# Attention and a feed-forward layer in one program: w_in's first half in two loads, fewer small matmuls and fp32 matmuls of zeros at the start, split 256-column matmuls in group 0, five chunks abreast in group 1

## The chip, the cores and the metric

The kernel runs on one core of one Trainium2 chip. The metric is the device time of one execution in microseconds; lower is better. Three timed runs of the kernel before took 325.07, 323.78 and 324.67 us (median 324.67). One more execution was recorded by the profiler.

## The reference

A block of attention with two paths, local and pooled, feeds a two-layer network with a gated activation.

```python
# attention: q, k, v are (8 batches, 8 heads, 576, 64)
q_d, k_d, v_d = (x.reshape(B, H, 144, 4, D).mean(axis=3) for x in (q, k, v))
out_d = softmax(scale * q_d @ k_d.T) @ v_d             # pooled, 144 x 144
out_up = np.repeat(out_d, 4, axis=2)                   # back to 576
mask = np.abs(pos[:, None] - pos[None, :]) < 4         # 7 neighbours
out_local = softmax(where(mask, scale * q @ k.T, -1e9)) @ v
x = (out_up + out_local).transpose(0, 2, 1, 3).reshape(4608, 512)
# network: w_in (512, 2048), w_out (2048, 512)
h = x @ w_in
out = (h * sigmoid(1.702 * h)) @ w_out                 # (4608, 512), float32
```

## The kernel before

The order of every instruction is written by hand (`manual_schedule`): each engine runs its instructions in the order of the program text, and waits on semaphores where a tile is not ready. The framework derives these waits from the regions that instructions read and write.

The 4608 tokens are worked in nine groups of 512 (`TG`). For each group, `mm1` (matmuls at L766, `hps_mm`) makes 16 chunks of 128 hidden units, each the sum of four products over the four blocks of 128 input channels (`dmc`); ScalarE applies SiLU (L777) from PSUM into `gT`. `mm2` (L846) then makes four blocks of 128 tokens, each the sum of 16 products with `w_out`; ScalarE scales them (L829) and SyncE stores them. The attention of batch g + 1 is woven into group g: a table of positions (`POS`, for group 0 `POS_0`) says ahead of which of the group's steps the pieces of `attention(b)` are issued. Each head pair hp fills block hp of the transposed activations, `xT[hp]`.

PSUM has three double tiles `PA[0..2]` (two banks each) and two single ones `PM[0..1]`; `PB` is `PA` in another order. `two` lists the six banks of `PA`, so `two[4]` and `two[5]` are the halves of `PA[2]`. `bank` in `mm1` names the bank of each chunk; the first `abreast` chunks of a group are made side by side, block by block, so that the last block of `xT` is needed late.

Batch 0's attention runs alone ahead of group 0 and in another form. GpSimd (POOL) issues the loads in this order, on one queue: k and q of batch 0, v in ten pieces (`load_vb`), `w_in` in two halves of 1024 columns (L239), k and q of batch 1, half of `w_out`, and later v of batch 1 and the rest. TensorE warms up with matmuls of zeros (`warm`, L733), makes local scores (L374) and pooled scores (L419) for head pairs 0/1 and then 2/3, pools v with selection matrices (`prep_vd_pe`, L339), and for each head pair multiplies the local weights with v (`av_local0`, L452) and the pooled ones with pooled v (`av_down0`, L468). VectorE divides by the sums (`normalise0`, L488 to L495). `turned` up-samples and transposes the result on TensorE (`transp_sum`, L510 and L527) and copies it into `xT` (`copy_x`). Between the turnings of head pairs stand the first matmuls of group 0's first product, written as `part(chunks, blocks)`: chunks 0 and 1 of block 0 behind the turning of pair 1, block 1 of the same chunks behind that of pair 2, and so on. A weight tile of chunk f takes every second column of 256 columns: chunks 0 and 1 read columns 0 to 255 of `w_in`.

In group 0's `mm2` the token blocks are worked in an order of their own: blocks 0 and 1 into `PM`, blocks 2 and 3 into the halves of `PB[0]`, four hidden chunks at a time. The pieces of batch 1's attention stand there at steps 0 (scores of the first head quad), 12 (scores of the second), 20 (`prep_vd_pe` for batch 1), 24, 33, 42 and 51 (`avx1` for each head pair, L557 and L569). For later batches pooled v comes from GpSimd (`prep_v4`, L311 and L314), from loads that SyncE issues, and `avx` (L634, L656) does two head pairs at once.

The functions that the change touches, and what calls them, follow with the line numbers of the profile.

Of the kernel before, what the change touches and what calls it, by code (L numbers as in the profile page):

```python
# [8 lines left out]
FP32 = mybir.dt.float32  # L9
# [6 lines left out]
TG = 512  # L16
# [3 lines left out]
def kernel(  # L20
# [9 lines left out]
    nc = tc.nc  # L30
# [207 lines left out]
    def load_w_in(c, n):  # L238
        nc.gpsimd.dma_start(  # L239
            out=w_in_bf[:, :, c : c + n],  # L240
            in_=bass.AP(
                tensor=moe_w_in.tensor, offset=moe_w_in.offset + c,
                ap=[[d_ff, 128], [128 * d_ff, n_dmc], [1, n]],
            ),
        )
# [213 lines left out]

    def av_down0(hp, o):  # L460
        Ed, vd, u = eds[hp // 2], vds[0], hp % 2
        blocks = [(0, 3)] + [(kc, c) for c in (0, 2) for kc in range(3)]
        for kc, c in blocks:
            rows, pos, slot, q0 = {
                0: (128, 0, 6, SD * kc), 2: (64, 1, 4, SD * kc + 128), 3: (64, 1, 5, 0),
            }[c]
            for j in range(2):
                nc.tensor.matmul(  # L468
                    o[64 * pos : 64 * pos + rows, j, 65 * slot : 65 * slot + 65],
                    lhsT=Ed[64 * j : 64 * j + 48, u, q0 : q0 + rows],  # L470
                    rhs=vd[64 * j : 64 * j + 48, kc, hp, :],
                    start=(kc == 0), stop=(kc == 2 or c == 3),
                    tile_position=(64 * j, 64 * pos),
                )

# [8 lines left out]
    def normalise0(o, y, parts="ab"):  # L484
        yl, yd, rc = y
        ov = o[:, :, 0:455].rearrange("p x (c e) -> p x c e", e=65)
        c0, c1 = {"a": (0, 4), "b": (4, 7), "ab": (0, 7)}[parts]
        nc.vector.reciprocal(rc[:, :, c0:c1], ov[:, :, c0:c1, 64:65])  # L488
        if "b" in parts:
            nc.vector.tensor_tensor(  # L490
                out=yd.rearrange("p s x d -> p x s d"), in0=ov[:, :, 4:7:2, 0:D],
                in1=rc[:, :, 4:7:2].to_broadcast([128, 2, 2, D]), op=ALU.mult,
            )
            c1 = 6
        nc.vector.tensor_tensor(  # L495
            out=yl[:, :, c0:c1], in0=ov[:, :, c0:c1, 0:D],
            in1=rc[:, :, c0:c1].to_broadcast([128, 2, c1 - c0, D]), op=ALU.mult,
        )
# [231 lines left out]
    def warm(n, cols=512, t=None):  # L730
        t = pm_tile() if t is None else t
        for _ in range(n):
            nc.tensor.matmul(  # L733
                t[:, 0:cols], lhsT=wz[:, 0:128], rhs=wz[:, 0:cols], start=True, stop=True
            )

    def attention(b):
        st = {}

        def s_pe(qd):  # L740
            P = PB if b == 1 else PA
            st["d", qd], st["s", qd] = scores_mixed(b, qd, P)

        def s_act(qd):
            if qd == 0:
                nc.scalar.preload_act_table_set("natural_log_exp_and_others")
            if qd:
                exp_down(qd, st["d", qd])
            exp_local(qd, st["s", qd], (1, 0) if qd else (0, 1))
            if not qd:  # L750
                exp_down(qd, st["d", qd])
            mask_local(qd)

        def s1():
            s_pe(1)
            s_act(1)

        first = [lambda: s_pe(0), lambda: s_act(0), s1]
        if b == 1:
            return first + [lambda hp=hp: avx1(b, hp) for hp in range(HP)]  # L760
        return first + [lambda: avx(b, (0, 1)), lambda: avx(b, (2, 3))]
# [1 line left out]
    w_in_v = w_in_bf.rearrange("p c (f i u) -> p c f u i", u=2, i=128)  # L763

    def hps_mm(g, ffc, dmc, acc):
        nc.tensor.matmul(  # L766
            acc,
            lhsT=w_in_v[:, dmc, ffc // 2, ffc % 2, :],
            rhs=xT[dmc][:, g * TG : g * TG + TG],
            start=(dmc == 0), stop=(dmc == n_dmc - 1),  # L770
        )

    def new_gT():
        return moe_sb.tile([128, n_ffc, TG], BF16, name="gT", tag="gT")
# [6 lines left out]
    def mm1(g, gT, steps):  # L781
        two = [PA[i][:, u, :] for i in range(3) for u in range(2)]
        bank, abreast = [PM[0], two[0], PM[1], two[2], two[4]], 4
        if g == 0:
            bank = acc[0:6] + late
        elif g == 1:
            bank, abreast = [two[0], two[2], two[1], two[3], PM[1], PM[0]], 6
            bank = bank + [two[4], two[5], two[0], two[2]] + PM + PM + PM
        else:
            bank = bank + bank + PM + PM + PM  # L790
        for ffc in range(n_ffc):
            for f in steps.get(ffc, ()):
                f()
            if g and ffc < abreast:
                if ffc == 0:
                    for dmcs in ((0, 1), (2,), (3,)):
                        for u in range(abreast):
                            for dmc in dmcs:
                                hps_mm(g, u, dmc, bank[u])
            elif g or ffc > 5:  # L800
                for dmc in range(n_dmc):
                    hps_mm(g, ffc, dmc, bank[ffc])
            else:
                continue
            silu(gT, ffc, bank[ffc])

    def mm2(g, gT, steps):
# [28 lines left out]
        for t, ffc in order:  # L836
            if g == n_groups - 1 and t == 3:
                continue
            for f in steps.get(n, ()):
                f()  # L840
            n += 1
            if ffc == 0:
                ops[t] = PB[0][:, t - 2, :] if g == 0 and t > 1 else pm_tile()
            wide = d_model // 2 if g == 0 and t > 1 and ffc > 7 else d_model
            for c in range(0, d_model, wide):
                nc.tensor.matmul(  # L846
                    ops[t][:, c : c + wide],
                    lhsT=gT[:, ffc, t * 128 : (t + 1) * 128],
                    rhs=w_out_bf[:, ffc, c : c + wide],
                    start=(ffc == 0), stop=(ffc == n_ffc - 1 and c + wide == d_model),  # L850
                )
            if ffc == n_ffc - 1 and not (g == 0 and t == 2):
                for u in (2, 3) if g == 0 and t == 3 else (t,):
                    store(u, ops[u], 0, d_model, nc.scalar, nc.sync)
# [35 lines left out]
    fill()  # L890
    for i in range(5):
        load_vb(0, i)
    load_w_in(0, 1024)
    load_w_in(1024, 1024)
    for qd in range(NQ):
        load_qk(1, qd)
# [17 lines left out]
    reduce_qk(0, 1, "k")  # L914
    reduce_qk(0, 1, "q")
    warm(6)
    warm(10, 128)
    exp_down(0, scores_d(0, 0, PA[2]))
    sp = scores(0, 1, barred=True, sp=PA[0:2])
    exp_local(1, sp)  # L920
# [1 line left out]
    for hp in range(4):  # L922
# [1 line left out]
        y[hp] = y_tiles0()  # L924
    prep_vd_pe(
        0, PM[0], range(0, 2),
        between=lambda kc, i: warm({(1, 2): 1, (1, 3): 2}.get((kc, i), 0), t=PM[1]),
    )
    for hp in range(2):
        av_local0(hp, o[hp], range(4))  # L930
# [1 line left out]
    sd = scores_d(0, 1, PB[2])  # L932
    prep_vd_pe(0, PM[1], range(2, 3))
    exp_down(1, sd)
    warm(2, t=PM[0])
    nc.scalar.preload_act_table_set("silu_and_others")
    for hp in range(3):
        av_local0(hp, o[hp], range(4 if hp < 2 else 0, 5))
        av_down0(hp, o[hp])
        normalise0(o[hp], y[hp], "b" if hp < 2 else "ab")  # L940
    make_mask()

    gT0 = new_gT()
# [100 lines left out]
```

## Time and profile before

| | |
|---|---|
| timed runs | 323.78, 324.67, 325.07 us |
| profiled execution | 323.4 us |
| its span, first to last instruction | 321.6 us |
| matmuls busy (PE) | 309.9 us, 96% of the span |
| ScalarE (ACT) busy | 203.1 us, 63% |
| VectorE (DVE) busy | 146.9 us, 46% |
| GpSimd (POOL) busy | 149.5 us, 46% |
| mean granted TensorE clock | 0.988 |
| all DMA | 39.96 MB, mean 124 GB/s |

How to read the rows. A row of the timeline has the start of a run of like instructions, its length, the engine, the source line, the operation, output and inputs, the shape and the count; a bracket at its end holds the idle time of that engine just before the row and what ended it. "issue" stands where the profile shows nothing that the engine waited for. PEld is TensorE's weight load, which overlaps its matmuls. Matmuls are pipelined: the next starts before the one before has ended, so the length of one is more than its share of the time, and a gap between ends and starts is less than what start to start would show. A row of the table of stretches has the stretch, its length, then busy time and number of instructions of PE, PEld, DVE, ACT and POOL, the granted TensorE clock, the DMA share and GB/s. `pa` and `pm` are the tiles of `PA` and `PM`.

By stage: batch 0's attention fills TensorE's first 25 us; group 0 runs from there to about 65 us, with batch 1's attention within; from 74 us TensorE is busy without a gap of note until 300 us; the last group has no attention beside it and ends with the stores.

### The profile page before, as it was taken

The numbers are of one execution on the slowest core, as the hardware profiler recorded it, in microseconds if no ns is written. First come the engines' busy times: TensorE is split into PE (matmuls) and PEld (weight loads), VectorE is DVE, ScalarE is ACT, GpSimd is POOL, SyncE is SP. The second block draws the span as 40 slices with busy tenths as digits, with TensorE's granted clock in tenths as the row PEclk, the third lists the DMA queues.
The fourth block names the chain that finished last, engine by engine and source line by source line (L and its number), as shares of the span: only waits on it lengthen the run. The fifth ranks groups of instructions, "written<-read, shape, count | busy, mean of one in ns | idle before, by whom it ended". The sixth has DMA issues, their size and how long they took to land.

```text
span 321.6 us, 9884 instructions
## 1 busy us (share of the span) xinstructions
PE 309.9 (96%) x4303; PEld 156.7 (49%) x4303; DVE 146.9 (46%) x300; ACT 203.1 (63%) x324; POOL 149.5 (46%) x173
## 2 busy tenths in 40 slices
PE   8879998998999999999999999999999999999995
PEld 3554454644554555454545454445444544444444
DVE  6862922782279226922693269325941580000000
ACT  4452775575885688567857785778587857415611
POOL 8832380447512992299229932992299030000000
PEclk9995999999999999999999999999999999999999
DMA  7999999649933893379438942894240120020011
GB/s 124 119 207 211 169 145 211 120 154 204 192 111 115 172 204 105 106 169 198 124 99 178 196 122 89 176 194 123 91 137 2 42 93 2 0 98 35 0 65 65
DMA packets 62571, 39.96 MB, mean 124 GB/s; under 512 B 44608, under 2 KB 51904, under 8 KB 62528
## 3 DMA queue, kind: packets, MB, share of 16 engines
q0 software_dynamic: 17312, 14.95, 33.1%
q1 hardware_dynamic: 45072, 24.32, 29.0%
q8 instruction: 33, 0.54, 0.8%
q14 instruction: 10, 0.08, 0.1%
q10 hardware_dynamic: 144, 0.07, 0.1%
HBM read 44.83 MB, written 9.44 MB: 169 GB/s over the span
## 4 chain that ended last, share of the span: by engine, by line
PE 89%; DMA 6%; POOL 2%; ACT 1%; issue 1%; DVE 0%; POOLq 0%
PE pm L846 36%; PE pm L766 24%; PE pa L766 15%; DMA w_in_bf<-in_moe_w_in_dram 4%; PE pa L392 3%; PE pa L846 2%; PE pa L656 2%; DMA qb<-in_q_dram 2%; PE pa L634 2%; PE pa L419 2%; ACT gT L777 1%; PE pm L861 1%; POOL vb L216 1%; PE pa L569 1%; PE pa L557 0%
## 5 line engine op out<-in xcount | busy, mean ns | idle before, releaser
L846 PE MATMUL pm<-w_out_bf,gT 128*128 128x512 bf16 x528 | 119.6, 379 | 1.1 <-issue 1.1
L766 PEld LDWEIGHTS <-w_in_bf 128*128 128x128 bf16 x576 | 55.8, 98 | 69.3 <-issue 3.4
L766 PE MATMUL pm<-xT,w_in_bf 128*128 128x512 bf16 x348 | 89.0, 382 | 0.4 <-DMA w_in_bf<-in_moe_w_in_dram 0.4
L846 PEld LDWEIGHTS <-gT 128*128 128x128 bf16 x576 | 54.3, 98 | 62.4 <-issue 1.6
L777 ACT ACTIVATE gT<-pm 128x512 bf16<-128x512 f32 x87 | 52.1, 604 | 40.9 <-PE pm L766 40.9
L766 PE MATMUL pa<-xT,w_in_bf 128*128 128x512 bf16 x228 | 60.5, 381 | 2.1 <-ACT gT L777 2.1
L444 DVE TENSOR_TENSOR es<-es,mask 128x600 bf16<-128x600 bf16 x28 | 17.7, 668 | 92.7 <-ACT es L430 92.5
L829 ACT ACTIVATE osb<-pm 128x512 f32<-128x512 f32 (+2 forms) x35 | 20.3, 582 | 30.5 <-PE pm L846 28.0
L777 ACT ACTIVATE gT<-pa 128x512 bf16<-128x512 f32 x57 | 32.9, 608 | 8.6 <-PE pa L766 8.6
L726 POOL TENSOR_TENSOR xT<-xT,od 128x576 bf16<-128x576 bf16 x12 | 15.4, 1281 | 40.8 <-DVE xT L710 40.8
L710 DVE TENSOR_TENSOR xT<-n,l 128x285 bf16<-128x285 f32 (+1 forms) x96 | 28.1, 365 | 0.0
L294 POOL TENSOR_TENSOR pq<-kT 128x576 f32<-128x576 bf16 x11 | 12.7, 1157 | 30.4 <-DVE kT L263 30.4
L311 POOL TENSOR_TENSOR pq<-v 112x512 f32<-112x512 f32 x18 | 23.9, 1331 | 4.9 <-DMA v<-in_v_dram 4.9
L831 DVE TENSOR_SCALAR osb<-pm 128x128 f32<-128x128 f32 x1 | 0.3, 291 | 54.0 <-ACT osb L829 54.0
L216 POOL DMA_DIRECT2D vb<-in_v_dram x20 | 13.7, 698 | 16.4 <-DVE y L490 4.7
L430 ACT ACTIVATE es<-pa 128x600 bf16<-128x600 f32 x32 | 19.7, 669 | 1.8 <-PE pa L374 1.7
L263 DVE STREAM_TRANSPOSE kT<-kb 128x576 f32<-128x576 f32 x16 | 19.9, 1245 | 0.0
L263 DVE STREAM_TRANSPOSE qT<-qb 128x576 f32<-128x576 f32 x16 | 19.8, 1238 | 0.0
L436 ACT ACTIVATE ed<-pa 128x864 bf16<-128x864 f32 x16 | 14.3, 894 | 5.9 <-PE pa L419 5.9
L705 ACT ACTIVATE l<-l 128x1440 f32<-128x1440 f32 x12 | 16.9, 1404 | 0.4
L699 ACT ACTIVATE l<-pa 128x492 f32<-128x492 f32 x24 | 12.6, 578 | 6.0 <-PE pa L656 6.0
L700 DVE COPY n<-pa 128x492 f32<-128x492 f32 x24 | 15.0, 665 | 2.8 <-ACT l L699 2.2
(119 smaller groups left out, 361.2 us busy)
## 6 DMA issues: line engine op xcount, KB each, us to landing
out_dram<-osb SPq DMA_DIRECT2D x34, 256.0 KB, 2.0
vf<-in_v_dram SPq DMA_DIRECT2D x60, 128.0 KB, 5.3
v<-in_v_dram SPq DMA_DIRECT2D x72, 96.0 KB, 3.0
kb<-in_k_dram POOLq DMA_DIRECT2D x16, 288.0 KB, 6.6
qb<-in_q_dram POOLq DMA_DIRECT2D x16, 288.0 KB, 8.5
w_in_bf<-in_moe_w_in_dram POOLq DMA_DIRECT2D x2, 1024.0 KB, 11.7
w_out_bf<-in_moe_w_out_dram POOLq DMA_DIRECT2D x4, 512.0 KB, 13.6
vb<-in_v_dram POOLq DMA_DIRECT2D x20, 64.0 KB, 5.8
```

The costliest lines, as they stand in the source:

```text
L216: nc.gpsimd.dma_start(out=vbs[b % 2][64 * par : 64 * par + 64, i, :, 0:D], in_=bass.AP(tensor=v.tensor, offset=v[b, 0].offset + (114 * i + ...
L263: nc.vector.transpose(out=t32.rearrange("p (i c) -> p c i", c=18), in_=store[b, qd].bitcast(FP32).rearrange("p (c d) -> p c d", c=18),)
L311: eng.tensor_tensor(out=t1[0:112], in0=x[:, :, 0:2, :], in1=x[:, :, 2:4, :], op=ALU.add)
L430: nc.scalar.activation(out=es[2 * qd + u][:, :, 0:300], in_=sp[u][:, :, 0:300], func=AF.Exp, scale=inv_sqrt_d,)
L444: nc.vector.tensor_tensor(out=ev, in0=ev, in1=mask, op=ALU.mult)
L705: nc.scalar.activation(out=l, in_=l, func=AF.Exp, scale=-1.0)
L710: nc.vector.tensor_tensor(out=out, in0=sub(n, *part), in1=sub(l, *part), op=ALU.mult)
L726: eng.tensor_tensor(out=xs, in0=xs, in1=sub(od[:, u, :], 0, (1, SD), (0, 4)), op=ALU.add)
L766: nc.tensor.matmul(acc, lhsT=w_in_v[:, dmc, ffc // 2, ffc % 2, :], rhs=xT[dmc][:, g * TG : g * TG + TG], start=(dmc == 0), stop=(dmc == n_ ...
L777: nc.scalar.activation(out=gT[:, ffc, :], in_=acc, func=AF.Silu, scale=GELU_SCALE)
L829: eng.activation(out=osb, in_=ap, func=AF.Copy, scale=1.0 / GELU_SCALE)
L846: nc.tensor.matmul(ops[t][:, c : c + wide], lhsT=gT[:, ffc, t * 128 : (t + 1) * 128], rhs=w_out_bf[:, ffc, c : c + wide], start=(ffc == 0) ...
```

## The change

Seven edits, made together:

- `w_in`'s first half is loaded as two loads of 512 columns; the second half stays one load of 1024. Ten loads follow one place further back on GpSimd.
- `av_down0` makes 12 matmuls for head pairs 0 to 2 instead of 14: the separate pair for slot 5 (which only puts numbers where nobody has written) goes, and the three pairs for slot 4 write slot 5 with it (130 columns instead of 65). Pair 3 keeps 14.
- `warm(10, 128)`, `warm(2, t=PM[0])` and the three warming matmuls of 512 columns inside `prep_vd_pe` go.
- `fill_pe(n, t)` is new: n matmuls of zeros, with the zero tile read as fp32, 128 x 128 by 256 columns. One stands inside `prep_vd_pe`, two behind the third head pair's `av_down0`.
- In group 0 the first product's chunks 6, 7 and 8 make their blocks 1 to 3 as two matmuls of 256 columns each instead of one of 512.
- In group 0 the second product does the same for hidden chunks 8 to 15 of token blocks 0 and 1; blocks 2 and 3 did so before.
- Group 1 makes five chunks abreast instead of six, and chunk 5 onwards takes other banks: `PM[0], two[4], two[0], two[2], PM[1], PM[0], ...` instead of `PM[0], two[4], two[5], two[0], two[2], PM[0], ...`.

```diff
     def av_down0(hp, o):
         Ed, vd, u = eds[hp // 2], vds[0], hp % 2
-        blocks = [(0, 3)] + [(kc, c) for c in (0, 2) for kc in range(3)]
-        for kc, c in blocks:
-            rows, pos, slot, q0 = {
-                0: (128, 0, 6, SD * kc), 2: (64, 1, 4, SD * kc + 128), 3: (64, 1, 5, 0),
-            }[c]
+        last = hp == HP - 1
+        blocks = [(0, 5)] if last else []
+        blocks += [(kc, slot) for slot in (6, 4) for kc in range(3)]
+        for kc, slot in blocks:
+            rows, pos, q0 = (128, 0, SD * kc) if slot == 6 else (64, 1, SD * kc + 128)
+            n = 2 if slot == 4 and not last else 1
             for j in range(2):
                 nc.tensor.matmul(
-                    o[64 * pos : 64 * pos + rows, j, 65 * slot : 65 * slot + 65],
+                    o[64 * pos : 64 * pos + rows, j, 65 * slot : 65 * (slot + n)],
                     lhsT=Ed[64 * j : 64 * j + 48, u, q0 : q0 + rows],
-                    rhs=vd[64 * j : 64 * j + 48, kc, hp, :],
-                    start=(kc == 0), stop=(kc == 2 or c == 3),
+                    rhs=vd[64 * j : 64 * j + 48, kc, hp : hp + n, :],
+                    start=(kc == 0), stop=(kc == 2 or slot == 5),
...
+    def fill_pe(n, t):
+        z = wz.bitcast(FP32)
+        for _ in range(n):
+            nc.tensor.matmul(t[:, 0:256], lhsT=z[:, 0:128], rhs=z, start=True, stop=True)
+
...
     def hps_mm(g, ffc, dmc, acc):
-        nc.tensor.matmul(
-            acc,
-            lhsT=w_in_v[:, dmc, ffc // 2, ffc % 2, :],
-            rhs=xT[dmc][:, g * TG : g * TG + TG],
-            start=(dmc == 0), stop=(dmc == n_dmc - 1),
-        )
+        n = TG // 2 if g == 0 and 5 < ffc < 9 and dmc else TG
+        for c in range(0, TG, n):
+            nc.tensor.matmul(
+                acc[:, c : c + n],
+                lhsT=w_in_v[:, dmc, ffc // 2, ffc % 2, :],
+                rhs=xT[dmc][:, g * TG + c : g * TG + c + n],
+                start=(dmc == 0), stop=(dmc == n_dmc - 1 and c + n == TG),
+            )
...
         elif g == 1:
-            bank, abreast = [two[0], two[2], two[1], two[3], PM[1], PM[0]], 6
-            bank = bank + [two[4], two[5], two[0], two[2]] + PM + PM + PM
+            bank, abreast = [two[0], two[2], two[1], two[3], PM[1]], 5
+            bank = bank + [PM[0], two[4], two[0], two[2]] + PM[::-1] * 4
...
-            wide = d_model // 2 if g == 0 and t > 1 and ffc > 7 else d_model
+            wide = d_model // 2 if g == 0 and ffc > 7 else d_model
...
-    load_w_in(0, 1024)
+    load_w_in(0, 512)
+    load_w_in(512, 512)
     load_w_in(1024, 1024)
...
     warm(6)
-    warm(10, 128)
     exp_down(0, scores_d(0, 0, PA[2]))
...
     prep_vd_pe(
         0, PM[0], range(0, 2),
-        between=lambda kc, i: warm({(1, 2): 1, (1, 3): 2}.get((kc, i), 0), t=PM[1]),
+        between=lambda kc, i: fill_pe(int((kc, i) == (1, 3)), PM[1]),
     )
...
     exp_down(1, sd)
-    warm(2, t=PM[0])
     nc.scalar.preload_act_table_set("silu_and_others")
     for hp in range(3):
         av_local0(hp, o[hp], range(4 if hp < 2 else 0, 5))
         av_down0(hp, o[hp])
         normalise0(o[hp], y[hp], "b" if hp < 2 else "ab")
+    fill_pe(2, PM[0])
     make_mask()
```

## The prediction

> **What bounds the kernel now.** I read the page first, then TensorE's timeline to 80 us, then a table of stretches, then the rows of the loads and of the engines that release TensorE.
>
> ```profile
> span 321.6 us, 9884 instructions
> PE 309.9 (96%) x4303; PEld 156.7 (49%) x4303; DVE 146.9 (46%) x300; ACT 203.1 (63%) x324; POOL 149.5 (46%) x173
> ...
> q8 instruction: 33, 0.54, 0.8%
> ```
>
> TensorE sets the end. Its program is 4303 weight loads and 4303 matmuls. The instruction queue moved 0.54 MB in 33 pieces, 261 instructions a piece by division, so near 128 pairs of load and matmul. The gaps worth removing are the bracketed ones here:
>
> ```profile
> 14.36 0.49 PE L733 MATMUL pm<-wz 128*128 128x256 bf16 x3 [0.41 <-issue]
> ...
> 21.37 0.22 PE L452 MATMUL pa<-vb,es 64*64 64x65 bf16 x4 [1.74 <-issue]
> 21.40 0.22 PE L468 MATMUL pa<-vd,ed 48*64 48x65 bf16 x2
> ...
> 21.97 0.63 PE L510 MATMUL pm<-up,y 128*128 128x231 bf16 x4
> ...
> 22.92 0.35 PE L452 MATMUL pa<-vb,es 64*64 64x65 bf16 x18
> ...
> 23.65 0.69 PE L510 MATMUL pa<-up,y 128*128 128x231 bf16 x4
> ...
> 27.67 1.04 PE L766 MATMUL pm<-xT,w_in_bf 128*128 128x512 bf16 x2 [0.42 <-DMA w_in_bf<-in_moe_w_in_dram]
> ...
> 44.52 2.76 PE L846 MATMUL pm<-w_out_bf,gT 128*128 128x512 bf16 x12
> ...
> 48.26 0.60 PE L846 MATMUL pm<-w_out_bf,gT 128*128 128x512 bf16 x2
> 49.99 0.59 PE L846 MATMUL pm<-w_out_bf,gT 128*128 128x512 bf16 x2 [1.13 <-issue]
> 50.42 1.02 PE L846 MATMUL pa<-w_out_bf,gT 128*128 128x512 bf16 x4
> ...
> 70.68 1.03 PE L766 MATMUL pa<-xT,w_in_bf 128*128 128x512 bf16 x4
> 73.82 2.75 PE L766 MATMUL pa<-xT,w_in_bf 128*128 128x512 bf16 x12 [2.11 <-ACT gT L777]
> ```
>
> Three gaps have no releaser ("issue"). The table of stretches cut at them counts the matmuls between:
>
> ```profile
> 0.00:14.10 14.10, 11.57 (x223) 6.04 (x224) 11.33 (x34) 6.44 (x10) 12.28 (x28) 1.00 1.53 126
> 14.10:20.50 6.40, 5.28 (x128) 2.87 (x128) 4.20 (x10) 4.04 (x7) 4.12 (x7) 1.00 1.19 169
> 20.50:49.50 29.00, 27.07 (x384) 14.03 (x384) 14.31 (x20) 16.31 (x33) 13.04 (x17) 0.88 1.31 181
> ```
>
> 223, then 128, then 384 = 3 x 128. So I take "issue" to be TensorE at the end of one program piece, with the next not there; pieces end after matmuls 223 + 128k. A piece ends wherever the count says, so added and removed matmuls move the ends through the code. After a stall the next piece was there 21.37 - 14.36 = 7.0 us later; the piece after that lasted longer and cost nothing.
>
> The clock comes on top (the last three numbers of a row are granted clock, DMA share and GB/s):
>
> ```profile
> 17.27:24.10 6.83, 5.09 (x145) 3.35 (x134) 5.15 (x14) 3.92 (x8) 2.00 (x3) 1.00 1.12 210
> 24.10:27.51 3.41, 3.15 (x21) 1.68 (x21) 1.23 (x2) 0.98 (x4) 0.00 (x0) 0.50 1.12 211
> 27.51:30.92 3.41, 3.25 (x16) 1.57 (x17) 0.00 (x0) 0.54 (x3) 1.61 (x3) 0.50 1.11 211
> 71.89:78.71 6.82, 4.89 (x76) 2.33 (x77) 2.19 (x2) 4.64 (x9) 6.74 (x8) 1.00 0.94 196
> ```
>
> From 24.10 to 30.92 TensorE ran at half clock, after a stretch with 1.74 us idle and mostly small matmuls. The stretch around the 2.11 us gap, as idle but with dense matmuls, kept the full clock.
>
> The price list, start to start: a 512-column matmul (2.76 - 0.38)/11 = 0.216 us, taking 0.38 as the length of one; a 256-column one (0.49 - 0.27)/2 = 0.11. A gap counts about 0.17 more than its bracket, since TensorE could have started the next matmul 0.17 before the previous one's modelled end.
>
> **The change, part by part.**
>
> *w_in in three loads.* The chain of waits and the rows of the tile:
>
> ```profile
> L239 POOL DMA_DIRECT2D w_in_bf<-in_moe_w_in_dram x2: 792/798/803, 13.1 to 13.9; - x2
> ...
> DMA to landing us min/median/max: 9.6/11.7/13.8
> ...
> 13.86 13.76 DMA w_in_bf<-in_moe_w_in_dram
> ...
> 30.89 0.57 PE pa L766 x2
> ```
>
> The first half landed 9.6 us after 13.1, at 22.7; the second at 27.63. Yet what waits to 27.67 is the pair of block 1 for chunks 0 and 1, columns 0 to 255, which lie in the first half; the block 0 pair had run before the second half landed. So the wait covers more than the columns it needs: in each partition the second load spans from column 1024 of block 0 to the end of block 3, and block 1 lies between. All three new loads span block 1 too. I therefore expect the wait to remain, on the last third, and the split to give nothing. It costs one more issue on POOL (0.80 us), behind which the next k/q, w_out and v loads are issued; the transfers are queued behind each other, so their landing is set by the rate. Rates: 210 GB/s in the stretch of w_in, 126 in that of the small v packets (first row above). For 1 MB in halved packets the bounds are 0 and 8.3 - 5.0 = 3.3 us; I take 0.3, near the w_in end, as half-size packets are nearer to it. TensorE resumes at 27.97.
>
> *The start.* Out go 10 + 3 + 2 warming matmuls and 2 in each of three head pairs; in comes one fp32 matmul, later two. The 10 lie ahead of a wait for VectorE, the fp32 one ahead of a v load, and the third head pair behind ScalarE's reading of its bank:
>
> ```profile
> 11.73 0.58 PE L419 MATMUL pa<-qdT,kdT 32*64 32x144 bf16 x24 [0.64 <-DVE qdT L282]
> ...
> 16.35 0.11 PEld L339 LDWEIGHTS <-psel 128*64 128x64 bf16 x2 [0.45 <-DMA vb<-in_v_dram]
> ...
> 18.20 0.90 ACT L436 ACTIVATE ed<-pa 128x864 bf16<-128x864 f32 x1
> ```
>
> So nothing starts earlier up to 19.1. The piece that ended 14 matmuls into the third pair's 34 (the 371st ends it) now ends at 371 - 21 + 1 = 351, exactly behind it; TensorE does 0.6 us of work (21.37 to 21.97) before the stall instead of behind it. The fp32 matmuls stand at that edge. The trace has none; 256 fp32 columns are at least a 256-column bf16 matmul, 0.11, and I bound it above by four times a 512-column step at half clock, 4 x 2 x 0.216 = 1.7; value 0.45, two of them 0.9. The Trainium skill ("FP8 and Floating Point Precision", TensorE Precision Notes) says true FP32 takes four passes through the array; by it one is an estimated 4 x 0.11 = 0.44, and the sum would be the same. Even at the upper bound they are nearly covered: the work from 21.4 to the w_in wait (up-sampling and turning of pairs 0, 1, 2 at 22.92 - 21.97 = 0.95 each, the last pair's products at 23.65 - 22.92 = 0.73, two dense matmuls at 0.43) is 4.0 us at full clock, so TensorE reaches it at 25.4 and idles 2.5 us.
>
> What is gained is the clock. Before, 27.67 to 30.89 ran at half clock: four dense matmuls and the last turning, 3.22 us. At full clock they are 4 x 0.216 + 0.95 (21.97 to 22.92) = 1.81. With fewer idle us in 17 to 24 I expect full clock there: 3.22 - 1.81 - 0.3 = **1.1 us**. If not, -0.3.
>
> *Group 0's split matmuls.* 9 in the first product, 16 in the second; a pair of 256 columns is 2 x 0.11, so nothing, at most 25 x 0.01 = 0.2. But they and the start move the piece's end that cost 1.13: it stood two matmuls behind the scores, at 735; now 733 - 21 + 1 + 2 + 9 = 724 ends the scores, and 11 more fit, eight dense ones and three small instead of two dense: 6 x 0.216 + 0.2 = 1.5 us later in the code, against a loss of 1.13 + 0.17 = 1.3. The stall goes; next late is ScalarE's reading of the bank of the first `pa` product:
>
> ```profile
> 48.43 0.89 ACT L436 ACTIVATE ed<-pa 128x864 bf16<-128x864 f32 x1 [0.92 <-PE pa L419]
> ```
>
> It ends at 49.32, so that product starts at 49.37 instead of 50.42: **1.05 us** (0 to 1.3).
>
> *Group 1.* The seventh chunk's bank shares its PSUM tile with the eighth's:
>
> ```profile
> 70.23 2.06 ACT L777 ACTIVATE gT<-pa 128x512 bf16<-128x512 f32 x4 [1.64 <-PE pa L766]
> 72.15 1.12 ACT L777 ACTIVATE gT<-pm 128x512 bf16<-128x512 f32 x2
> 73.11 0.66 ACT L777 ACTIVATE gT<-pa 128x512 bf16<-128x512 f32 x1
> ```
>
> The seventh SiLU ends at 73.77 and TensorE starts at 73.82: the eighth chunk's writes wait for the reading of the same tile's other half. With five abreast, `two[0]`'s tile is complete at the group's 18th matmul (17 x 0.216 + 0.38 = 4.1 us after its start) instead of the 21st, SiLUs follow at 0.5 each, and the eighth chunk goes into `two[0]`: SiLU 0 to 2 are done at 5.6, TensorE asks behind 28 matmuls, at 6.05. The gap (2.28 start to start) goes. But what is fed by DMA does not come earlier by it:
>
> ```profile
> 87.23 0.84 POOL L314 TENSOR_TENSOR vd<-pq 112x256 bf16<-112x256 f32 x1
> ...
> 89.48 0.26 PE L634 MATMUL pa<-ed,vd 48*64 48x144 bf16 x4
> 89.56 0.23 PE L634 MATMUL pa<-ed,ones 48*64 48x144 bf16 x4
> ```
>
> The third block of pooled v is ready at 88.07 and needed 0.15 behind 89.48; moved up 2.28 that is 87.35, so 0.75 is lost again: **1.5 us** (1.3 to 2.28; -0.5 if the bank turns themselves wait).
>
> **The sum.** 1.1 + 1.05 + 1.5 = 3.65. The profiled execution took 323.4 (span 321.6 and 1.8 around it) and lies 1.3 below the median, 324.67; the mean of it and the three timed is 324.2. From 324.2: **320.6**; its own range 319.2 to 321.9.
>
> **The rivals.**
>
> - *The w_in wait is freed.* For: the first two loads land near 22.7. Against: block 1 waits on columns that it doesn't read. TensorE goes on at 25.4, 2.5 us more: 318.1.
> - *The clock stays half to 30.92.* For: less dense work in 10 to 17. The 1.1 becomes -0.3: 322.0.
> - *The half clock moves into the dense stage.* The 2.5 us idle ahead of w_in are one gap; if the gate answers at 30.92 and holds 6.83 us as before, 3.4 us of dense work are lost: 324.0. Against: the row 71.89:78.71. The Trainium skill ("TensorE: Matmul & The Clock Gate", Why this matters for your kernels) allows gaps up to about 3 us; by it no drop follows here. The trace half agrees: 2.11 did no harm, 1.74 among small matmuls did.
> - *A stall stays.* The program piece after 724 comes late, or group 1 waits elsewhere: one of 1.05 and 1.5 is lost, 321.9.
> - *Slower: the program ends meet the attention bursts.* All later ends shift by 6 pairs. Between 87.45 and 93.48, with two bursts, a piece lasted 6.0 us without a stall; at the 7.0 us seen at 21.37 it would lose 1.0 in each of six such groups: 326.6. It decides where a piece takes over 6.0 us to come. Against: transfers are lighter there.
>
> ```profile
> 87.45:93.48 6.03, 6.03 (x151) 3.16 (x138) 2.68 (x7) 5.01 (x8) 0.62 (x1) 1.00 0.56 137
> ```
>
> **How the numbers follow.** A measurement tells 0.5%, 1.6 us, from no change: faster is under 323.05, slower over 326.3. Forecast 0.41, w_in freed 0.09, clock half as before 0.14, a stall stays 0.12: faster 0.76. Clock in the dense stage 0.14: same. Program ends 0.10: slower. Range 318.4 to 324.2: it takes in all but the slower rival and half of the freed one's and the dense clock's spread; w_in's 3.3 us bound, taken as unlikely, ends within it (323.6).
>
> **What would show it.** Right: no "issue" gap near 48 to 50; no gap at L766 around 70; a w_in wait of 2 us or more ending near 28; granted clock 1.00 from there. Wrong: L766 going on before 26 (split works); clock 0.50 behind 28; new "issue" gaps behind 80; a long L634 wait on POOL is the 0.75 mis-sized.

## The result, and the profile after

| kernel | median us | runs | ratio to before, 95% |
|---|---|---|---|
| before | 324.97 (323.12 to 326.93) | 19 | |
| changed | 321.81 (318.56 to 324.05) | 19 | 0.9885 (0.986 to 0.991) |

The ratio is 3.7 us (2.9 to 4.5) off 324.97; the forecast's parts summed to 3.65. The total was met. The ratio and its interval, here and below, leave out the executions more than 1.5% above the fastest of the same kernel (here 2 of 19; 2 of 6 in two of the runs below), so the ratio is not that of the medians, 0.990. The profiled execution of the changed kernel took 322.18 us, with a span of 320.1. That is only 1.2 below the profiled one of before: in this execution one term of the sum, the clock, came out with the other sign.

TensorE's timeline of the changed kernel, from the third head pair to block 1 of the first product (columns: start, length, engine, line, instruction, count, idle before and who ended it). Every line number behind the down products is a few higher than before: L774 is the first product (L766 before), L854 the second (L846), L741 the fp32 matmul.

```profile
19.53 0.55 PE L469 MATMUL pa<-vd,ed 48*128 48x65 bf16 x11
21.38 0.26 PE L469 MATMUL pa<-vd,ed 48*64 48x130 bf16 x1 [1.30 <-issue]
21.58 2.07 PE L741 MATMUL pm<-wz 128*128 128x256 f32 x4
23.45 0.91 PE L511 MATMUL pm<-up,y 128*128 128x231 bf16 x4
...
27.41 0.61 PE L774 MATMUL pm<-xT,w_in_bf 128*128 128x512 bf16 x1
...
29.71 1.03 PE L774 MATMUL pm<-xT,w_in_bf 128*128 128x512 bf16 x2
```

The two fp32 matmuls appear as four: each is two pairs of load and matmul. They run behind the program stall, not inside it, and so does the last matmul of the third pair (21.38). They hold the first turning back from 21.58 to 23.45. The table of stretches (the last three numbers: granted clock, DMA share, GB/s) shows why they took that long:

```profile
17.57:20.98 3.41, 2.35 (x67) 1.66 (x64) 2.89 (x9) 3.14 (x4) 0.98 (x2) 1.00 1.23 200
20.98:24.39 3.41, 3.01 (x12) 1.94 (x12) 1.53 (x3) 0.00 (x0) 0.72 (x2) 0.50 1.13 212
24.39:31.22 6.83, 6.61 (x68) 3.67 (x68) 1.54 (x3) 2.29 (x9) 2.06 (x3) 0.50 1.12 211
```

In this execution the clock was half for 10.24 us, against 6.83 before. That is not typical of the changed kernel. In these traces half clock lasts 3.41 us or a multiple of it; call 3.41 us at half clock a lost window. One lowers the mean granted clock by 0.5 x 3.41 / 320 = 0.005, so the mean counts them: 0.995 is one, 0.984 three. Of the changed kernel's 19 executions 13 have 0.994 or more; of 62 executions of the kernel before, taken beside the experiments, 7 have. The profiled one, 0.984, is among the six that have less.

The same timeline around the score burst of group 0, and in group 1:

```profile
49.91 0.81 PE L854 MATMUL pm<-w_out_bf,gT 128*128 128x512 bf16 x3 [0.16 <-issue]
50.79 1.02 PE L854 MATMUL pa<-w_out_bf,gT 128*128 128x512 bf16 x4
52.13 0.97 PE L339 MATMUL pa<-vb,psel 128*64 128x256 bf16 x14 [0.32 <-ACT es L430]
...
69.43 1.03 PE L774 MATMUL pa<-xT,w_in_bf 128*128 128x512 bf16 x4
70.29 1.24 PE L774 MATMUL pm<-xT,w_in_bf 128*128 128x512 bf16 x5
71.37 2.75 PE L774 MATMUL pa<-xT,w_in_bf 128*128 128x512 bf16 x12
73.96 2.75 PE L774 MATMUL pm<-xT,w_in_bf 128*128 128x512 bf16 x12
...
87.91 0.26 PE L635 MATMUL pa<-ed,vd 48*64 48x144 bf16 x4
```

The 1.13 and the 2.11 are gone. At the pooling matmuls (L339) 0.32 is left, which the row puts down to ScalarE's exp; the part on the prediction reads it as the rest of the stall instead. (The 0.16 ahead of the x3 is the place of a matmul without a record: the page counts 4272 matmuls and 4313 weight loads.) Group 1 runs back to back (5 x 0.216 from 70.29 to 71.37, 12 x 0.216 to 73.96). The products at L635 have no wait on GpSimd.

The rows of w_in's loads:

```profile
L239 POOL DMA_DIRECT2D w_in_bf<-in_moe_w_in_dram x3: 747/767/776, 13.3 to 15.0; - x3
...
DMA to landing us min/median/max: 8.0/9.8/13.8
```

The last third landed at 15.0 + 13.8 = 28.8, against 27.6 before. TensorE reached block 1 only at 29.71, so nothing waited for it here.

### The profile page after: what moved, and what is told of

Read it like the earlier page. It is cut to its first block, busy times and chain, and to the rows that moved or that the text cites. A ratio compares the mean times of both kernels' runs of the same rounds, so it can differ in the third digit from the quotient of the medians.

```text
span 320.1 us, 9864 instructions
## 1 busy us (share of the span) xinstructions
PE 305.1 (95%) x4272; PEld 160.0 (50%) x4313; DVE 146.6 (46%) x300; ACT 203.0 (63%) x324; POOL 151.5 (47%) x174
## 4 chain that ended last, share of the span: by engine, by line
PE 91%; POOL 2%; issue 2%; DMA 2%; ACT 1%; DVE 0%; POOLq 0%; DVEq 0%; ACTq 0%
PE pm L854 35%; PE pm L774 24%; PE pa L774 16%; PE pa L392 3%; PE pa L657 2%; PE pa L854 2%; DMA vb<-in_v_dram 2%; PE pa L419 2%; PE pa L635 2%; PE pm L869 1%; POOL vb L216 1%; PE pm L741 1%; PE pa L469 1%; PE pa L511 1%; PE pa L570 1%
## 5 line engine op out<-in xcount | busy, mean ns | idle before, releaser
L854 PE MATMUL pm<-w_out_bf,gT 128*128 128x512 bf16 (+1 forms) x521 | 114.9, 373 | 3.2 <-issue 3.0
L774 PEld LDWEIGHTS <-w_in_bf 128*128 128x128 bf16 x585 | 56.6, 98 | 65.6 <-issue 0.7
L774 PE MATMUL pm<-xT,w_in_bf 128*128 128x512 bf16 (+1 forms) x344 | 87.7, 378 | 0.4
L854 PEld LDWEIGHTS <-gT 128*128 128x128 bf16 x592 | 55.9, 98 | 60.2 <-issue 0.6
L774 PE MATMUL pa<-xT,w_in_bf 128*128 128x512 bf16 (+1 forms) x225 | 59.0, 378 | 0.4
L785 ACT ACTIVATE gT<-pa 128x512 bf16<-128x512 f32 x56 | 32.1, 609 | 6.3 <-PE pa L774 6.3
L727 POOL TENSOR_TENSOR xT<-xT,od 128x576 bf16<-128x576 bf16 x12 | 16.7, 1396 | 38.0 <-DVE xT L711 37.7
L430 ACT ACTIVATE es<-pa 128x600 bf16<-128x600 f32 x32 | 19.7, 669 | 1.8 <-PE pa L374 1.7
L216 POOL DMA_DIRECT2D vb<-in_v_dram x20 | 13.7, 696 | 13.9 <-DMA w_in_bf<-in_moe_w_in_dram 6.0
```

The costliest lines, as they stand in the source:

```text
L216: nc.gpsimd.dma_start(out=vbs[b % 2][64 * par : 64 * par + 64, i, :, 0:D], in_=bass.AP(tensor=v.tensor, offset=v[b, 0].offset + (114 * i + ...
L430: nc.scalar.activation(out=es[2 * qd + u][:, :, 0:300], in_=sp[u][:, :, 0:300], func=AF.Exp, scale=inv_sqrt_d,)
L727: eng.tensor_tensor(out=xs, in0=xs, in1=sub(od[:, u, :], 0, (1, SD), (0, 4)), op=ALU.add)
L774: nc.tensor.matmul(acc[:, c : c + n], lhsT=w_in_v[:, dmc, ffc // 2, ffc % 2, :], rhs=xT[dmc][:, g * TG + c : g * TG + c + n], start=(dmc = ...
L785: nc.scalar.activation(out=gT[:, ffc, :], in_=acc, func=AF.Silu, scale=GELU_SCALE)
L854: nc.tensor.matmul(ops[t][:, c : c + wide], lhsT=gT[:, ffc, t * 128 : (t + 1) * 128], rhs=w_out_bf[:, ffc, c : c + wide], start=(ffc == 0) ...
```

## The experiments

All were timed in five rounds beside the kernel before, whose median was 324.4 to 324.7 each time.

**Group 1's bank turns alone**, on the kernel before:

```
-            bank, abreast = [two[0], two[2], two[1], two[3], PM[1], PM[0]], 6
-            bank = bank + [two[4], two[5], two[0], two[2]] + PM + PM + PM
+            bank, abreast = [two[0], two[2], two[1], two[3], PM[1]], 5
+            bank = bank + [PM[0], two[4], two[0], two[2]] + PM[::-1] * 4
```

> The kernel before with group 1's bank turns alone (five chunks abreast). Theory (the parts add up; the bank gap of 2.28 us start to start is worth all of itself): 2.3 us faster than before, about 322.7 beside 325.0; the row of L766 behind the fifth-to-eighth chunk shows no idle on ScalarE, and the L634 row near 87 shows no wait on GpSimd. Rival (0.75 is lost again at the pooled v of GpSimd): 1.5 us faster, with a wait of about 0.7 on POOL at L634.

321.99 us, ratio 0.9918 (0.9891 to 0.9945): 2.7 us (1.8 to 3.5). Its timeline and GpSimd's:

```profile
70.15 1.24 PE L766 MATMUL pm<-xT,w_in_bf 128*128 128x512 bf16 x5
71.23 2.75 PE L766 MATMUL pa<-xT,w_in_bf 128*128 128x512 bf16 x12
...
87.75 0.26 PE L634 MATMUL pa<-ed,vd 48*64 48x144 bf16 x4
...
88.02 0.23 PE L634 MATMUL pa<-ed,vd 48*64 48x144 bf16 x4
```
```profile
87.07 0.73 POOL L314 TENSOR_TENSOR vd<-pq 112x256 bf16<-112x256 f32 x1
```

The third block of pooled v is ready at 87.07 + 0.73 = 87.80 and needed 0.27 behind the first row of L634, at 88.02: no loss here. By the time the theory holds and the rival, 1.5, does not. The row alone would not settle it, since L634 starts only 89.48 - 87.75 = 1.73 earlier than before, not 2.28: this execution came to group 1 later (its scores for batch 1 start at 43.95, before at 43.47).

**The 25 split matmuls alone**, on the kernel before:

```
+        n = TG // 2 if g == 0 and 5 < ffc < 9 and dmc else TG
...
-            wide = d_model // 2 if g == 0 and t > 1 and ffc > 7 else d_model
+            wide = d_model // 2 if g == 0 and ffc > 7 else d_model
```

> The kernel before with its 25 split matmuls of group 0 alone (9 in the first product, 16 in the second). Theory (program pieces of 128 load-and-matmul pairs): the piece that ended two matmuls behind the score burst now ends 9 earlier in the code, 7 matmuls ahead of the burst's end. TensorE stalls inside the burst until about 50, ScalarE's exp of that burst starts about 1.7 us later than 48.43, and the kernel is 0.5 to 1.0 us slower than before. Rival (the splits themselves remove the stall): no issue gap near 48 to 50, and 0.65 to 1.05 us faster. Second rival (the splits are only split): no change, gap of 1.13 where it was.

326.84 us, ratio 1.0078 (1.0057 to 1.0099): 2.5 us slower. The timeline of TensorE, ScalarE's, and the table of stretches:

```profile
50.79 0.22 PE L392 MATMUL pa<-qT,kT 32*64 32x60 bf16 x3 [2.10 <-issue]
50.99 1.35 PE L848 MATMUL pm<-w_out_bf,gT 128*128 128x512 bf16 x4
52.14 1.91 PE L848 MATMUL pa<-w_out_bf,gT 128*128 128x512 bf16 x4
53.98 1.43 PE L339 MATMUL pa<-vb,psel 128*64 128x256 bf16 x14
```
```profile
51.17 0.89 ACT L436 ACTIVATE ed<-pa 128x864 bf16<-128x864 f32 x1 [3.21 <-PE pa L419]
```
```profile
48.60:50.70 2.10, 0.09 (x11) 0.00 (x0) 0.00 (x0) 0.00 (x0) 0.15 (x1) 1.00 1.09 205
50.80:54.20 3.40, 3.40 (x19) 1.19 (x20) 0.85 (x2) 2.02 (x3) 0.00 (x0) 0.61 1.11 216
```

The stall lies inside the score burst, seven matmuls ahead of its end, as counted; the sign and the place were right, the size was not (0.5 to 1.0 was expected). The stall is 2.10 instead of 1.13, and the stretch behind it has a granted clock of 0.61: eight dense matmuls take 53.98 - 50.99 = 2.99 us instead of 8 x 0.216 = 1.73.

**The start alone** (w_in in three loads, the shorter down products, the exchanged matmuls of zeros; splits and banks as before):

> The changed start alone (w_in's first half in two loads, down products in 12 matmuls, zero matmuls removed and fp32 ones added), group 0 and group 1 as before. An fp32 matmul counts two load-and-matmul pairs, so 21 pairs go out and 6 come in. Theory: the piece ends at 735 + 15 = 750 in the count of before, among the small pooling matmuls; the issue gap near 48 to 50 is gone (0.65 us gained), but the start itself gives nothing or loses (the fills stand behind the stall at 21.4 and the last w_in load lands about 1 us later): between 0.65 faster and 0.8 slower in all. Rival (the prediction's: the clock stays full from 28 on, 1.1 gained): 1.7 us faster in all, granted clock 1.00 from 28.

323.75 us, ratio 0.9981 (0.9951 to 1.0011): 0.6 us faster (-0.4 to 1.6), not told from no change, as the theory had it; the rival's 1.7 lies just outside. Its timeline and stretches:

```profile
22.88 0.60 PE L772 MATMUL pm<-xT,w_in_bf 128*128 128x512 bf16 x2
...
27.42 0.61 PE L772 MATMUL pm<-xT,w_in_bf 128*128 128x512 bf16 x2 [3.08 <-DMA w_in_bf<-in_moe_w_in_dram]
...
72.72 4.44 PE L772 MATMUL pa<-xT,w_in_bf 128*128 128x512 bf16 x12 [2.11 <-ACT gT L783]
```
```profile
27.90:29.30 1.40, 1.40 (x11) 0.81 (x9) 0.00 (x0) 0.00 (x0) 0.70 (x2) 0.79 1.11 211
...
72.70:77.00 4.30, 4.28 (x13) 1.57 (x13) 0.28 (x1) 1.19 (x2) 4.22 (x5) 0.60 1.03 178
```

TensorE idles 3.08 us ahead of block 1, as the prediction's step on w_in had it (2.5 there), but the clock falls behind this wait (0.79 granted from 27.90 to 29.30); and the 2.11 gap of group 1, harmless in the execution of before, here cost the clock too: its 12 matmuls took 4.44 us instead of 2.75. There is no issue gap near 48 to 50.

**Ten zero matmuls fewer**, on the kernel before:

```
     warm(6)
-    warm(10, 128)
     exp_down(0, scores_d(0, 0, PA[2]))
```

> The kernel before without the ten 128-column matmuls of zeros that stand ahead of the first down scores; nothing else. Theory (pieces are counted in matmuls): the piece ends at 735 + 10 = 745 in the count of before, among the pooling matmuls, the issue gap of 1.13 near 50 goes, 0.65 to 1.05 us faster; the gap of 1.74 near 21 stays, ten matmuls later in the code (behind 24 of the third pair's 34). Rival (the zeros are needed for the clock): half clock in more than the 6.83 us from 24 to 31, no change or slower.

322.98 us, ratio 0.9968 (0.9937 to 0.9999): 1.0 us. Its timeline:

```profile
49.47 0.41 PE L339 MATMUL pa<-vb,psel 128*64 128x256 bf16 x4
50.14 0.75 PE L339 MATMUL pa<-vb,psel 128*64 128x256 bf16 x10 [0.25 <-issue]
```

The rest of the stall stands behind the fourth pooling matmul. By the rows of before the burst ends at 733, eight dense matmuls follow and then the pooling ones, so the stall stands at 733 + 8 + 4 = 745 in the count of before: moved from 735 by exactly the ten that were left out. With the splits' run, where it moved by exactly nine, this shows that the stalls follow the count.

**The parts of w_in and of the fills**, each on the changed kernel. First w_in's first half in one load again, then, as a run of its own, the two fills behind the third pair (`fill_pe(2, PM[0])`) left out. The first edit:

```
-    load_w_in(0, 512)
-    load_w_in(512, 512)
+    load_w_in(0, 1024)
```

> The changed kernel with w_in's first half in one load again. Theory (all loads are waited for together, so the split only adds an issue and smaller packets): w_in's last part lands 0.3 to 1.1 us earlier (27.6 instead of 28.76), the first product of group 0 never goes on to input block 1 before the last landing, and the time is 0 to 1.1 us below the changed kernel's 321.8, so 320.7 to 321.8. Rival (the split lets TensorE start earlier): 1 us or more slower than the changed kernel, 322.8 and up.

> The changed kernel without the two fp32 matmuls of zeros behind the third head pair. Theory: they stand behind the program stall and not in it, but the wait for w_in covers them, so where TensorE reaches w_in before its last landing nothing changes, and where it comes late 0.9 to 1.9 us are gained: between 0 and 1 us faster than 321.8 in the median; four pairs fewer move the piece end near the score burst 4 matmuls later in the code, among the pooling matmuls, at no cost. Rival (they hold the clock): half clock lasts longer in the stretch 20 to 34, 0.5 to 1.7 us slower.

320.61 us, 0.9887 (0.9845 to 0.9929), and 320.11 us, 0.9873 (0.9841 to 0.9904), beside the changed kernel's 0.9885: neither is told from it. The split gives nothing that the time resolves. Without the fills no execution of 6 has a mean clock over 0.989, and yet the time is not longer: the rival is right about the clock, the theory about the time.

**w_in by blocks of input rows**, on the changed kernel, and then without the two fills as well:

```
-            out=w_in_bf[:, :, c : c + n],
+            out=w_in_bf[:, d : d + n, :],
...
-    load_w_in(0, 512)
-    load_w_in(512, 512)
-    load_w_in(1024, 1024)
+    for d in range(4):
+        load_w_in(d, 1)
```

> The changed kernel with w_in loaded by block of input rows (four loads of one block, all columns) instead of by columns. Theory (each load then writes a range that no other load spans, so a matmul of block 0 or 1 waits for its own load only): L774 goes on from block 0 to block 1 before 25, no wait of 2 us or more on w_in, the scores of batch 1 start 1.5 to 3 us earlier than 43.5 to 44.9, and the kernel takes 318.5 to 320. Rival (TensorE is late by itself, by clock and stall, and the last block's landing near 28 binds all the same): within 0.7 us of 321.8.

> As the run before it, with the two fp32 matmuls behind the third head pair left out too. Theory: with the wait for w_in gone nothing covers them any more, so leaving them out gains 0.9 (full clock) to 1.9 us (half clock) on top: 317 to 319. Rival (they hold the clock): not faster than the run before, with half clock in more windows between 20 and 34.

317.62 us, 0.9775 (0.9742 to 0.9807): 7.3 us off the kernel before, twice the changed kernel's 3.7. And 319.62 us, 0.9836 (0.9788 to 0.9883), without the fills. Five of 6 executions with them have a clock of 0.994 or more, two of 6 without: the rival was right about the clock. The theory's gain of 0.9 to 1.9 did not come; whether leaving them out costs time stays open, as the two intervals overlap. The timeline and stretches of the first, and one stretch of the second:

```profile
24.01 0.61 PE L774 MATMUL pm<-xT,w_in_bf 128*128 128x512 bf16 x2
...
24.92 0.55 PE L528 MATMUL pa<-id,y 128*128 128x114 bf16 x7
25.40 0.60 PE L774 MATMUL pm<-xT,w_in_bf 128*128 128x512 bf16 x2
```
```profile
20.60:24.00 3.40, 3.40 (x60) 2.48 (x60) 2.33 (x6) 0.76 (x3) 0.71 (x1) 1.00 1.08 218
24.00:27.50 3.50, 3.50 (x33) 2.07 (x31) 0.74 (x1) 1.71 (x7) 1.23 (x2) 1.00 1.04 203
```
```profile
20.60:24.00 3.40, 3.18 (x54) 2.16 (x53) 2.70 (x7) 1.35 (x4) 0.71 (x1) 0.70 1.08 217
```

With the fills block 1 follows the third turning without a wait, at full clock; without them the clock falls from 21.99, behind the place where they stood (0.70 in the stretch).

**The same three loads, each into a tile of its own**, against **the changed kernel with the banks of before**, which keeps the common tile:

```
+    w_in_bf = {
+        c: persist.tile([128, n_dmc, n], BF16, name=f"w_in{c}")
+        for c, n in ((0, 512), (512, 512), (1024, 1024))
+    }
...
-            out=w_in_bf[:, :, c : c + n],
+            out=w_in_bf[c],
```

> The changed kernel with its three w_in loads as they are (same columns, same packets, same order), but each into an SBUF tile of its own. Theory (the wait for the last load came from the range that a strided load spans in the common tile): chunks 0 and 1 go on to block 1 right behind the second turning, no wait for w_in of 1 us or more, the scores of batch 1 start before 42.5, and the kernel takes 316.8 to 318.6, as with loads by block. Rival (the blocks gained by longer packets, or TensorE needs the columns of the last load anyway): 320.5 to 322.

> The changed kernel with the bank turns of before in group 1, so the changed start and the splits together. Theory (the splits cost 2 us by themselves only because they move a piece end into the score burst; with the 15 pairs fewer of the start it falls at 741 in the count of before, behind the burst): 323.7 to 324.5, no issue gap between 47 and 51, and the 2.11 gap ahead of the eighth chunk's matmuls is back. Rival (the splits cost 2 us wherever the pieces end): 325.5 to 326.5.

Own tiles: 319.03 us, 0.9807 (0.9743 to 0.9871). Old banks: 323.13 us, 0.9947 (0.9916 to 0.9977). In both timelines TensorE reaches the first product at the same time; the first fence is that of the own tiles, the second that of the common one:

```profile
24.56 0.61 PE L782 MATMUL pm<-xT,w_in 128*128 128x512 bf16 x2
...
25.95 0.60 PE L782 MATMUL pm<-xT,w_in 128*128 128x512 bf16 x2
```
```profile
24.57 0.61 PE L774 MATMUL pm<-xT,w_in_bf 128*128 128x512 bf16 x2
...
26.96 0.61 PE L774 MATMUL pm<-xT,w_in_bf 128*128 128x512 bf16 x2 [0.94 <-DMA w_in_bf<-in_moe_w_in_dram]
```

Same loads, same columns, and the banks of group 1 come only later: the common tile makes block 1 wait, here for 26.96 - 25.95 = 1.0 us. With own tiles the last third landed at 14.7 + 12.4 = 27.1, so block 1 ran at 25.95 ahead of it, as in the run by blocks, whose last load landed at 15.2 + 13.7 = 28.9. In time the own tiles are 2.5 us better than the changed kernel (0.9807 against 0.9885, intervals that just overlap), the median a little above the 316.8 to 318.6 expected; the 1.0 is what the rows show of it.

As for the old banks, start and splits together are 1.7 us (0.7 to 2.7) faster than before, although the splits alone are 2.5 slower, and no issue gap stands near the burst: the splits' price is the place of the piece end, and the start moves it away.

**Is the rest of the change needed?** The kernel before with w_in by blocks, the new banks and the ten zeros fewer (the three edits shown above; no fp32 fills, no shorter down products, no splits):

> The kernel before with three edits: w_in loaded by blocks of input rows, group 1's new bank turns, and the ten 128-column zero matmuls left out (which moves the piece end off the score burst). No 12-matmul down products, no fp32 fills, no 256-column splits. Theory (of the change only the banks and the place of the piece end are worth time, and the freed w_in wait adds its own 3 to 4 us): 316.8 to 318.6, about what the changed kernel with w_in by blocks takes (317.6). Rival (the fp32 fills and the shorter down products hold the clock and are needed): 319.5 to 321.5, with half clock for two windows or more between 17 and 34.

319.44 us, 0.9854 (0.9819 to 0.9888), and all six executions at 0.988 or 0.989. The theory falls, the rival holds: here two windows are lost every time, and the interval lies above that of the changed kernel with blocks. Which of the parts left out does it this run does not say. Its table of stretches:

```profile
20.60:24.00 3.40, 3.40 (x67) 2.41 (x67) 2.85 (x7) 0.99 (x4) 0.71 (x1) 0.85 1.06 213
24.00:27.50 3.50, 3.50 (x17) 1.52 (x18) 0.29 (x1) 1.53 (x6) 0.88 (x2) 0.50 1.08 210
```

**Does it have to be fp32?** The changed kernel with w_in by blocks, each fp32 matmul replaced by two bf16 ones:

```
-        z = wz.bitcast(FP32)
-        for _ in range(n):
-            nc.tensor.matmul(t[:, 0:256], lhsT=z[:, 0:128], rhs=z, start=True, stop=True)
+        warm(2 * n, t=t)
```

> The changed kernel with w_in by blocks, and with each fp32 matmul of zeros replaced by two bf16 ones of 512 columns (the same two load-and-matmul pairs, 2 x 0.216 = 0.43 us at full clock, so the same length and the same piece ends). Theory (any work in that place holds the clock): the same as with the fp32 fills, 317 to 319, mean granted clock 0.994 or more in most runs. Rival (fp32 counts for more in the clock than bf16): half clock for two windows, 0.989 or less in most runs, 319 to 321.

317.70 us, 0.979 (0.9755 to 0.9824), all six executions at 0.995 or 1.0: no difference in time or clock. This and the fp32 run by blocks are the fastest here.

## Why the prediction was right, and where its steps failed

*Total.* 3.65 was forecast; 3.7 (2.9 to 4.5) came. Apart, the runs give 1.7 for start and splits (0.7 to 2.7; forecast 1.1 + 1.05 = 2.15) and 2.7 for group 1 (1.8 to 3.5; forecast 1.5). Only group 1 is off by more than its interval. It was forecast too low, and the rows below show that part of the other terms did not come, so the sum is better than its terms: that is luck.

*Group 1.* The mechanism was right: the eighth chunk's writes waited for the reading of the other half of the tile, and the gap went. The term that was mis-sized is the 0.75 "lost again" at the pooled v. It took the moment at which the third block is ready, 88.07, as fixed. It was 87.80 in the run of the banks alone, ahead of the need, and in the kernel with w_in by blocks, where these products start at 82.45 instead of 89.48, it is earlier as well:

```profile
82.37 0.73 POOL L314 TENSOR_TENSOR vd<-pq 112x256 bf16<-112x256 f32 x1
```
```profile
82.45 0.26 PE L635 MATMUL pa<-ed,vd 48*64 48x144 bf16 x4
...
83.16 0.26 PE L635 MATMUL pa<-ed,vd 48*64 48x144 bf16 x4 [0.26 <-POOL vd L314]
```

So that moment is not fixed (83.10 instead of 88.07); what remains there is a wait of 0.26, against the 0.75 of the forecast. The gap can also be dearer than its 2.28: in one of the five profiles that have it (the start alone) it took the clock with it.

*The stall at the score burst.* The count of 128 pairs and the direction of the shift were right. The step that failed is the price of the fp32 matmul in pairs: it counts two, so 15 pairs went out net at the start, not 18. The end lies three matmuls earlier in the code than written: behind the eight dense matmuls, right ahead of the pooling ones. By the prediction's own sum that is 6 x 0.216 = 1.3 later in the code against a loss of 1.3, with nothing to spare. What sets the length of such a stall (2.10 in the splits' run, 1.13 before) was not tried and stays open. ScalarE's exp of the burst starts at 48.43 before and at 49.85 after:

```profile
49.85 0.89 ACT L436 ACTIVATE ed<-pa 128x864 bf16<-128x864 f32 x1 [0.92 <-PE pa L419]
```

The product into `pa` comes 50.42 - 48.43 = 1.99 behind it before, 50.79 - 49.85 = 0.94 after: the 1.05 that was forecast, with the next late releaser named rightly. But 0.38 of it is lost at the pooling matmuls, which stand 2.95 behind the exp before and 2.28 after. The first row is of before, the second of the kernel with w_in by blocks, which has the same group 0:

```profile
51.38 0.97 PE L339 MATMUL pa<-vb,psel 128*64 128x256 bf16 x14
```
```profile
46.71 0.97 PE L339 MATMUL pa<-vb,psel 128*64 128x256 bf16 x14
```

There the exp starts at 44.82, and the pooling 46.71 - 44.82 = 1.89 behind it: the whole 1.05 came. It also starts ahead of the end of the two exps of L430 that follow (45.60 + 1.23 = 46.83), so it does not wait for the last of them. In the changed kernel's profile both had ended at 50.63 + 1.23 = 51.86, the first of them at 51.30, and the pooling started at 52.13. That the wait is the rest of the stall is a reading; the place is where the count puts the piece end.

*The clock.* "Full clock behind 28" was wrong of the profiled execution, where the rival "clock stays half" came: the clock fell at 20.98, ahead of the two fills. Of all executions 13 of 19 lose one window at most, against 7 of 62 before; where that window lies only a profile shows, and that of the old banks, with the same start, has the forecast path: block 0 at 24.57, a wait to 26.96, no half clock at all (mean 1.0).

What keeps the clock is shown in part. The counts point to the fills behind the third pair: without them, 0 of 6 and 2 of 6 executions have 0.994 or more, with them 13 of 19 and 5 of 6. For the kernels by blocks the profiles show it at that place. For the changed kernel they don't: without the fills its clock fell at 16.21 already, within a wait for v and ahead of the place where they stood. And of the start alone, which has the fills too, only 2 of 12 have 0.994 or more; in its profile the clock held until 28.71 and fell behind the wait for w_in and again behind the gap of group 1.

What the clock is worth was not timed by itself. The two executions of the changed kernel at 1.0 (median 320.8) beat the six below 0.994 (322.4) by 1.6, near the 1.4 that the forecast puts between full and half clock. But the eleven between scatter from 318.6 to 323.4, and without the fills the time was no longer though the clock was lost. Of the 1.7 for start and splits, 0.67 to 1.05 is the stall's, so 0.7 to 1.0, uncertain by 1.0 either way, is left for the 1.1: neither confirmed nor excluded.

*w_in.* That the split gives nothing, and why, is confirmed by the two timelines of the own and the common tile: the prediction's reading, that the wait covers the range a strided load spans. The rival "w_in freed", 318.1, is about what the kernel with blocks then did: 317.6. The wait itself, 2 us or more by the forecast's signs, varies: 3.08 in the start alone, 0.94 with the old banks, none in the profiled execution of the changed kernel, which came too late for it. The last landing was 1.1 later in the profile of after, not 0.3, but that is not the split's price: with the same three loads it was at 26.9 (old banks), 27.1 (own tiles) and 27.4 (start alone), against 27.6 with two loads before.

*The fills.* "Exactly behind" the third pair the piece does not end: at two pairs for an fp32 matmul it ends one matmul earlier, and the fills run behind the stall. Where the clock holds, the wait for w_in covers them, as forecast (0.94 of it is left in the run of the old banks). In the profiled execution of the changed kernel they took from 21.58 to 23.45 at half clock, and TensorE came to block 1 at 29.71, 0.9 behind the last landing, so there they were covered in part only. The Trainium skill ("FP8 and Floating Point Precision", TensorE Precision Notes) has true FP32 in four passes, an estimated 0.44 us. The rows of the kernels by blocks agree: two fp32 matmuls take 1.13, four bf16 ones of 512 columns, 4 x 0.216 plus the tail, 1.04.

```profile
20.43 1.13 PE L741 MATMUL pm<-wz 128*128 128x256 f32 x4
```
```profile
20.98 1.04 PE L734 MATMUL pm<-wz 128*128 128x512 bf16 x4
```

*The slower rival.* It did not come behind 80: in the table of waits of the changed kernel (us in total, times, longest) the second product's issue waits are 0.2 at most, the place of one matmul without a record.

```profile
PE pm L854 <- issue: 3.0, 19, 0.2
```

Its shift was miscounted: the later ends lie 25 - 18 = 7 pairs earlier in the code by the prediction's own count, not 6, and 25 + 6 - 21 = 10 with two pairs for each fp32 matmul (4313 weight loads against 4303). But its mechanism is real: where the splits alone put a piece end 9 pairs earlier, inside a burst, 2.5 us were lost; with the start's 15 out the end near that burst lies 6 later, and both together gain.

## What to carry to other kernels

Count load-and-matmul pairs to each "issue" gap before adding or removing small matmuls: an edit that costs nothing by itself can move a program end into a burst that another engine waits for, or out of it. When a matmul waits for a load whose columns it doesn't read, look at the range that the strided load spans; load along the tile's outer dimension, or into tiles of their own, rather than in smaller pieces. A timing whose executions differ in the granted clock needs several runs a side; one profile may show the unlucky one, and the mean clock alone does not give the time.

## What the runs showed of the hardware that was not expected

- The granted clock fell behind gaps of 2.10 us (splits alone, 0.61 in the next 3.4 us) and 2.11 us (start alone, 0.60 in the next 4.3 us) ahead of dense matmuls. The same 2.11 gap did nothing in the profile of before, nor in that of the old banks, whose row is below. The Trainium skill ("TensorE: Matmul & The Clock Gate", Why this matters for your kernels) allows gaps up to about 3 us; the first two speak against that as a safe bound, and the prediction's 0.14 for a drop in the dense stage rested too much on one harmless gap.

```profile
70.86 2.75 PE L774 MATMUL pa<-xT,w_in_bf 128*128 128x512 bf16 x12 [2.11 <-ACT gT L785]
```

- An fp32 matmul is two load-and-matmul pairs in the trace (two appear as four) and in the count of the program (10 weight loads more in all, as 25 + 6 - 21).
- In fills of equal length, bf16 zeros held the clock as well as fp32 ones (1.0 in five of 6 executions, against four of 6).
